# The second expert's second product as seven products of halves, with a new instruction order

## Chip, core and metric

The kernel runs on one core of one Trainium2 chip. The metric is device time in microseconds (us), the median of several executions. TensorE (PE in the rows) multiplies, with its weight loads shown apart as PEld; VectorE (DVE), ScalarE (ACT) and GpSimd (POOL) do the elementwise work; SyncE's queue (SP) issues every DMA.

## The reference

A linear attention without softmax, a root mean square norm over heads, and two feed-forward experts, one behind the other, over 4608 tokens of width 512. The first expert has an inner width of 2048, the second of 1024.

```
kv  = einsum('bhsd,bhse->bhde', k, v)
out = einsum('bhsd,bhde->bhse', q, kv)
x   = out / sqrt(mean(out*out) + 1e-6) * g_norm        # then to (4608, 512)
h   = x @ w_in;   x = (h * cos(h)) @ w_out             # first expert, d_ff 2048
h   = x @ w_in2                                        # second expert, d_ff 1024
e   = exp(h - max(h));  solu = h * e / (sum(e) + 1e-9)
ln  = (solu - mean) / sqrt(var + 1e-6) * g_ln
out = ln @ w_out2
```

All of it is fp32. The kernel splits each operand of a large product into a high part, rounded to the matmul's format, and a low part, the rest; `mm3` (lines 170 to 173) makes a product of three matmuls: high by high, high by low, low by high. Each matmul comes with a weight load of 128x128.

## The kernel before

**Products of halves.** Several products are made by seven products of halves in place of eight (Winograd's form): the left operand is cut into A11, A12, A22 and the sums S1 to S4, the right one into B11, B21, B22 and the sums T1 to T4, and the results are added from PSUM. Before the change this holds for the first expert's first product and for the second expert's first product (`second`), not for the second expert's second product (`second_out`).

**Stages.** Attention and a first quarter of the first expert run interleaved in blocks of 512 tokens (36 steps, `step_h` and `step_out`). Then the other three quarters of the first expert run in blocks of 3 or 4 tiles of 128 tokens per half (`first_h`, `first_out`), so that their moving operand has 384 or 512 columns. Meanwhile jobs (`job_in`, `job_out`, `job_b`, `job_lw`) decode the weights, which arrive as 64-bit words, split them and spill the parts to DRAM. Then comes the second expert, 18 pairs of tiles of 128 tokens:

- `prep_second` loads the pair and forms the sums of halves on POOL (`prep`), the high parts on ACT and the low parts on DVE.
- `second`: 42 matmuls of 512 columns, copied and added into `h2` by ACT and DVE.
- `soft`, for each of the two rows: maximum (DVE), exponential (ACT), product (DVE), square (ACT), a power on POOL, scaling (DVE).
- `second_out`, for each row: 8 transposes of 128 columns by TensorE, high parts on ACT (line 1017), low parts on DVE (line 1020), then 24 matmuls of 512 columns against `rg` 0 to 7, which hold the weights from `lwd`; one copy (ACT, line 1034) and one DMA out.

**What sets the order.** All work is given to a planner (`Flow`) as tasks with an engine, a duration, what they read and write, and a due time `at`. `Flow.run` lays them out in time by those numbers and emits each engine's instructions in that order. On the chip every engine runs its own list in order and waits on semaphores, so a duration in the table moves instructions, and a wait at the head of an engine's list holds all behind it.

```
s, eng = min((min(start(t) for t in q), e) for e, q in ready.items() if q)
t = min((t for t in q if start(t) <= s), key=lambda t: (t.at, t.seq))
t.end = self.free[eng] = s + t.dur
```

The code of the parts that the change touches:

Of the kernel before, what the change touches and what calls it, by code (L numbers as in the profile page):

```python
# [8 lines left out]
F32 = mybir.dt.float32  # L9
# [8 lines left out]
P = 128  # L18
# [27 lines left out]
POW = 2.0  # L46

BLOCKS = (0, 3), (6, 3), (12, 4), (20, 4), (28, 4)
E2_JOBS = (0, 0, 0, 0, 0, 0, 2, 3, 0, 2, 3, 0, 1, 1, 0)
PREP_LEAD, PREP_D, H_LATE, H_EARLY, JOB_AT = 12, 3, 0.3, 0.6, 10  # L50
T0, STEP_A, ITEM = 25.0, 8.0, 42.0
SLOTS0, SLOT_T, SLOT_D, SLOT_LATE, SLOT_RATE, JOB0, JOB1 = 8, -12, 1, -16, 2.0, 5, 32
CV_AHEAD, W_LOAD = 15, (-18.5, -12.5, -9, 6, 10, 14, 18, 22)
MM4, MM2 = 0.68, 0.36
GAP, PE_LAT = 0.04, 0.26
XPRI = 10
ATT_LEAD, CV_LEAD, Q_LEAD, PRI = 8, 14, 16, 20
KV_T = 0.62
PAIR_C, TR_LAG, OUT_LAG = 22.3, 20.0, 31.0
# [7 lines left out]
class Flow:  # L67
# [53 lines left out]
    def run(self):  # L121
        ready = {}
        port = 0.0

        def release(t):
            t.ready = 0.0
            for d in t.deps:
                gap = d.lat + (GAP if d.eng != t.eng or t.eng not in ("PE", "SP") else 0.0)
                if d.eng == "PE" and t.eng != "PE":
                    gap += PE_LAT  # L130
                t.ready = max(t.ready, d.end + gap)
            ready.setdefault(t.eng, []).append(t)

        def start(t):
            return max(self.free.get(t.eng, 0.0), t.ready, port if t.port else 0.0)
# [8 lines left out]
        for _ in self.tasks:  # L144
# [4 lines left out]
            t.end = self.free[eng] = s + t.dur  # L149
            if t.port:  # L150
                port = t.end
# [8 lines left out]
def tile_kernel(ctx, tc, qkv, tail, g2, w1, w2, gl, out):  # L160
# [26 lines left out]
    lwd = dram.tile([NC, P, 2, 512], F32, name="lwd")  # L187


    for key in ("g2", "halfpi"):  # L190
        declare("const", key, 0, [P, 1])
# [5 lines left out]
    declare("edge", "edge", 0, [P, 40])  # L197
    for s in range(2):
# [29 lines left out]
    declare("e2a", "xb", 2, [P, KC, TB])  # L228
# [9 lines left out]
    declare("e2t", "su", 6, [P, 512])  # L238
# [79 lines left out]
    def lhl(s):  # L318
        return buf["rwo", s].rearrange("p (l c n) -> p l c n", l=2, c=NC)
# [14 lines left out]
    hvs = Ring(("hv", i) for i in range(4))  # L334
    tts = Ring(("tt", i) for i in range(3))
# [16 lines left out]
    def convert(src, sk, yk, wk, at, load_at, on_dve, wide=1.3):  # L352
# [27 lines left out]
    def either(on_dve, n, fn, r, w, at):  # L380
        eng = DVE if on_dve else POOL
        dur = e_(0.82, 0.5, n) if on_dve else e_(1.38, 0.8, n)
        add("DVE" if on_dve else "POOL", dur, lambda: fn(eng), r=r, w=w, at=at)

    def split(src, keys, n, hi, lo, hk, lk, at, on_dve, scale=None):
# [8 lines left out]
        add("ACT", 0.64 if n == 512 else 0.42, lambda: ACT.copy(out=hi(), in_=src()), r=keys, w=hk, at=at)  # L394
# [91 lines left out]
    def kv_pair(b, bk, p, w, at):  # L486
# [12 lines left out]
        if b == 0:  # L499
            q_load(j, at + 3, Q_CUTS)  # L500
        add("PE", KV_T, mm, r=[kv, tl] + ([bk] if p % 2 else []), w=w + ([] if p % 2 else [bk]), at=at)

    def kv_slots(b):
        n, bks = ("kvf", b % 2), [att_bank() for _ in range(2)]

        def slot(half):
            def run(at):
# [4 lines left out]
                for e in range(2):  # L512
# [6 lines left out]
                    add("ACT", 0.35, copy, r=[bk, *done] + ([n] if half or e else []),  # L519
# [24 lines left out]
    def first_block(at, step):  # L544
# [4 lines left out]
        for p in range(NPAIR):  # L549
# [4 lines left out]
            for e in range(2):  # L554
                r, col = slice(e * D, (e + 1) * D), slice(p * P + e * D, p * P + (e + 1) * D)
                add("ACT", 0.26, lambda r=r, col=col, p=p: ACT.copy(
# [9 lines left out]
            add("PE", 0.45, mm, r=[kvf, ("kvfp", p, 0), ("kvfp", p, 1), q, ("qp", q, 0)], w=[bk], at=t)  # L566
            add("ACT", 0.61, lambda sq=sq, bk=bk: ACT.activation(out=buf[sq], in_=buf[bk], func=AF.Square, scale=D ** -0.5),
# [727 lines left out]
```

## Time and profile before

| | |
|---|---|
| median of 3 runs | 1279.22 us (1276.19 to 1279.84) |
| profiled execution, whole time | 1274.1 us |
| profiled execution, span of the core | 1272.3 us |
| mean granted TensorE clock | 0.999 |
| busy: PE, PEld, DVE, ACT, POOL | 98%, 83%, 72%, 53%, 40% |

The rows further down come from that one execution, whose whole time is 1.8 us above its span. A matmul's row shows its start and a modelled duration, which overlaps the next one; the distance from start to start says how fast they follow one another. A row's bracket names idle time before it and what ended it.

### The profile page before, as it was taken

Reading aid. Unit: us, or ns where it says so; the run is one execution under the profiler, and the core shown is the slowest. Engines: PE = TensorE matmul, PEld = TensorE weight load, DVE = VectorE, ACT = ScalarE, POOL = GpSimd, SP = SyncE. Lnnn points to the kernel's source line nnn. Section 1 sums busy time; section 2 is a strip of 40 time slices with the busy share of each in tenths; the row PEclk is TensorE's granted clock in tenths of the full one; section 3 lists DMA queues with packets and bytes.
Section 4 is the critical chain, followed back from the end, with each engine's and each line's share of the span. In section 5 each row is a group of like instructions: output and inputs, shape, how many; then the busy total and the mean of one; then the engine's idle time right before and its main releaser. Section 6 shows DMA issues by size and latency. Waiting matters only on the chain.

```text
span 1272.3 us, 18770 instructions
## 1 busy us (share of the span) xinstructions
PE 1241.3 (98%) x6576; PEld 1058.1 (83%) x6576; DVE 914.8 (72%) x1544; ACT 680.0 (53%) x1233; POOL 510.2 (40%) x510
## 2 busy tenths in 40 slices
PE   6799999999999999999999999999999999999998
PEld 4578888878999999888888888887888888888887
DVE  5777676787877777877788866656867776777753
ACT  4666766765564563555455534523655455455543
POOL 3237556665654764763463443322321212121000
PEclk9999999999999999999999999999999999999999
DMA  8779899577957857674865474396211111111000
GB/s 288 242 271 305 285 320 324 184 252 235 308 205 217 270 200 235 228 257 125 251 219 180 129 239 133 114 307 197 67 50 58 42 50 50 42 50 42 26 25 34
DMA packets 177407, 224.60 MB, mean 177 GB/s; under 512 B 11424, under 2 KB 114848, under 8 KB 177312
## 3 DMA queue, kind: packets, MB, share of 16 engines
q1 hardware_dynamic: 177312, 223.39, 54.0%
q8 instruction: 52, 0.85, 0.3%
q14 instruction: 43, 0.35, 0.1%
HBM read 156.77 MB, written 66.58 MB: 176 GB/s over the span
## 4 chain that ended last, share of the span: by engine, by line
PE 88%; DVE 3%; POOL 3%; DMA 2%; ACT 2%; issue 1%; SPq 0%; ACTq 0%; POOLq 0%; DVEq 0%
PE ps L171 27%; PE ps L173 27%; PE ps L172 27%; PE ps L1014 2%; PE ps L613 2%; POOL att L540 1%; PE ps L495 1%; DMA wid<-ws 1%; DMA px<-fh 1%; PE ps L645 1%; DMA att<-qkv 1%; POOL att L539 0%; POOL fconv L377 0%; POOL ws L395 0%; ACT xf L651 0%
## 5 line engine op out<-in xcount | busy, mean ns | idle before, releaser
L171 PE MATMUL ps<-rg,rwo 128*128 128x512 f32 (+1 forms) x912 | 347.2, 381 | 2.5 <-ACT fh L790 1.3
L173 PE MATMUL ps<-rg,rwo 128*128 128x512 f32 (+1 forms) x912 | 344.8, 378 | 1.2 <-DVE rwo L395 1.2
L172 PE MATMUL ps<-rg,rwo 128*128 128x512 f32 (+1 forms) x912 | 344.6, 378 | 1.0 <-DVE rg L755 1.0
L758 POOL TENSOR_TENSOR rg<-fh,rg 128x512 fp32r<-128x512 f32 (+1 forms) x120 | 146.0, 1230 | 141.9 <-ACT rg L753 124.7
L171 PEld LDWEIGHTS ps<-rg,rwo 128*128 128x128 f32 x912 | 171.2, 188 | 30.5 <-ACT fh L790 1.7
L173 PEld LDWEIGHTS ps<-rg,rwo 128*128 128x128 f32 x912 | 171.2, 188 | 30.0 <-DVE rwo L395 1.6
L172 PEld LDWEIGHTS ps<-rg,rwo 128*128 128x128 f32 x912 | 171.3, 188 | 28.9 <-DVE rg L755 1.3
L996 POOL TENSOR_TENSOR const<-const,const 128x1 f32<-128x1 f32 x36 | 21.1, 587 | 329.8 <-DVE const L993 244.9
L171 PE MATMUL ps<-rxa,rwi 128*128 128x512 f32 (+1 forms) x384 | 146.2, 381 | 1.4 <-DVE fh L944 0.9
L173 PE MATMUL ps<-rxa,rwi 128*128 128x512 f32 (+1 forms) x384 | 144.3, 376 | 0.0
L172 PE MATMUL ps<-rxa,rwi 128*128 128x512 f32 (+1 forms) x384 | 144.2, 376 | 0.0
L747 ACT ACTIVATE fh<-fh,const 128x512 f32<-128x512 f32 (+1 forms) x156 | 106.3, 691 | 40.0 <-DVE fh L744 39.3
L742 ACT ACTIVATE fh<-ps 128x512 int32<-128x512 f32 (+1 forms) x126 | 71.4, 568 | 104.6 <-PE ps L173 79.1
L171 PE MATMUL ps<-rxb,rwi 128*128 128x512 f32 (+1 forms) x288 | 110.8, 385 | 0.4 <-DVE fh L751 0.4
L172 PE MATMUL ps<-rxb,rwi 128*128 128x512 f32 (+1 forms) x288 | 108.4, 376 | 0.0
L173 PE MATMUL ps<-rxb,rwi 128*128 128x512 f32 (+1 forms) x288 | 108.3, 376 | 0.0
L744 DVE SCALAR_TENSOR_TENSOR fh<-ps,fh 128x512 f32<-128x512 f32 (+1 forms) x126 | 81.5, 648 | 29.6 <-ACT fh L742 27.8
L683 POOL TENSOR_TENSOR sf<-xf 128x256 f32<-128x256 f32 x72 | 63.8, 893 | 64.9 <-DMA xf<-xd 34.0
L890 DVE TENSOR_TENSOR mid<-ps,mid 128x512 f32<-128x512 f32 (+1 forms) x90 | 56.9, 635 | 43.7 <-PE ps L173 42.2
L395 POOL TENSOR_TENSOR ws<-fconv,ws 128x512 fp32r<-128x512 f32 (+1 forms) x52 | 65.9, 1271 | 44.8 <-ACT ws L394 40.2
L171 PEld LDWEIGHTS ps<-rxa,rwi 128*128 128x128 f32 x384 | 72.1, 188 | 13.2 <-DVE fh L944 1.4
L377 POOL TENSOR_TENSOR fconv<-fconv 128x512 f32<-128x512 f32 x40 | 53.3, 1333 | 73.8 <-DVE fconv L375 68.4
(134 smaller groups left out, 2377.1 us busy)
## 6 DMA issues: line engine op xcount, KB each, us to landing
rwi<-wid SPq DMA_DIRECT2D x66, 512.0 KB, 5.2
rwo<-wod SPq DMA_DIRECT2D x88, 256.0 KB, 3.5
fconv<-w SPq DMA_DIRECT2D x36, 512.0 KB, 5.4
att<-qkv SPq DMA_DIRECT2D x32, 512.0 KB, 6.7
px<-fh SPq DMA_DIRECT2D x42, 256.0 KB, 3.9
xd<-xf SPq DMA_DIRECT2D x18, 512.0 KB, 3.9
wid<-ws SPq DMA_DIRECT2D x18, 512.0 KB, 4.6
xf<-xd SPq DMA_DIRECT2D x18, 512.0 KB, 5.3
```

The costliest lines, as they stand in the source:

```text
L171: PE.matmul(ps, lhsT=lh, rhs=rh, start=start, stop=False, skip_group_check=more)
L172: PE.matmul(ps, lhsT=lh, rhs=rl, start=False, stop=False, skip_group_check=more)
L173: PE.matmul(ps, lhsT=ll, rhs=rh, start=False, stop=stop, skip_group_check=more)
L377: either(on_dve, 512, lambda eng: eng.tensor_tensor(out=buf[wk], in0=buf[yk], in1=buf[wk], op=ALU.add), r=[yk, wk], w=[wk], at=at)
L395: either(on_dve, n, lambda eng: eng.tensor_tensor(out=lo(), in0=src(), in1=f(hi()), op=ALU.subtract), [*keys, *hk], lk, at)
L613: PE.matmul(buf[bk][row:row + n, c], lhsT=buf[qs[p]][:, a:a + n], rhs=buf[kvf][:, c], start=True, stop=True)
L683: add("POOL", 0.9, lambda: POOL.tensor_tensor(out=out_(), in0=in0(), in1=in1(), op=fn), r=[*keys, *r], w=w, at=at)
L742: add("ACT", e_(0.61, 0.42, n), lambda: ACT.activation(out=tt().bitcast(I32), in_=h(), func=AF.Copy, scale=INV_2PI, bias=0.25), r=r, w=[tk ...
L744: add("DVE", e_(0.71, 0.44, n), lambda: DVE.scalar_tensor_tensor(out=tt(), in0=h(), scalar=INV_2PI, in1=tt().bitcast(I32), op0=ALU.mult, o ...
L747: add("ACT", e_(0.74, 0.5, n), lambda: ACT.activation(out=tt(), in_=tt(), func=AF.Sin, bias=buf["halfpi"][:, 0:1], scale=TWO_PI), r=[tk, " ...
L758: either(on_dve, n, lambda eng: eng.tensor_tensor(out=lo(), in0=g(), in1=f(hi()), op=ALU.subtract), [*gk, *hk], lk, t + 2)
L890: add("DVE", e_(0.71, 0.44, n), lambda ak=ak, bk=bk: DVE.tensor_tensor(out=buf[ak][:, 0:n], in0=buf[bk][:, 0:n], in1=buf[ak][:, 0:n], op=A ...
```

## The change

**The second product.** `second_out` now takes a pair of rows at once. The eight blocks of 128 of the inner dimension are cut into two halves of four, the columns into two halves of 256, and the two tiles of tokens are the halves of the rows. After the 16 transposes (as many as before) ACT copies one block of four from PSUM and DVE forms four sums S1 to S4 into buffers `e`; then seven operands get high parts (ACT) and low parts (DVE for A11, A12 and A22, POOL for the four sums). Seven products of 4 x 3 matmuls of 256 columns follow, 84 in all for 48 of 512 columns, and five adds (DVE) and two copies (ACT) of 256 columns put the result together.

**What feeds it.** `job_lw` makes the seven right-hand parts: 4 jobs for 8, each with two decodings, four scalings on ACT, the differences on POOL and four spills in place of two. The weights take 14 loads of 512 KB in place of 8, into `rg`, the new pool `e2r` and `ws`.

**Elsewhere.** The low parts in `prep_second` move from DVE to POOL; two small DVE operations of `soft` become one on ACT; one small ACT operation with a sine is put at the program's start and one with an exponential ahead of the second expert, each of which loads its table there.

**The order.** The planner's durations are set anew, most of them lower; `SLACK` multiplies them by 1.1 (DVE 1.11), `OVER` lets an operation start a little before the end of the one ahead, and POOL and DVE no longer exclude each other on the port but lengthen each other. Due times move too. All engines' lists change in all stages.

```diff
-PREP_LEAD, PREP_D, H_LATE, H_EARLY, JOB_AT = 12, 3, 0.3, 0.6, 10
+PREP_LEAD, PREP_D, H_LATE, H_EARLY, JOB_AT = 4.22, 3, 0.24, 0.31, 8.01
-MM4, MM2 = 0.68, 0.36
-GAP, PE_LAT = 0.04, 0.26
+MM4, MM2 = 0.68, 0.355
+GAP, PE_LAT, PORT = 0.04, 0.16, 0.58
+SLACK = {"DVE": 1.11, "ACT": 1.1, "POOL": 1.1}
+OVER = {"DVE": 0.084, "ACT": 0.104, "POOL": 0.042}
...
-            t.end = self.free[eng] = s + t.dur
+            t.end = s + t.dur * SLACK.get(eng, 1.0)
...
-             lambda part, lo, hi: e2xs(i)[:, part, 2 * lo:2 * hi, :], ("xsh", i), ("xsl", i), at, lambda n: True)
+             lambda part, lo, hi: e2xs(i)[:, part, 2 * lo:2 * hi, :], ("xsh", i), ("xsl", i), at, lambda n: False)
...
-        for c in range(NC):
-            add("PE", 0.7, lambda c=c: mm(c), r=[("lhq", n, c // 4), ("llq", n, c // 4), ("lw", c)] + ([bk] if c else []),
-                w=[bk], at=at)
...
+        add("ACT", 0.59, lambda: ACT.copy(out=total(S3), in_=a(1, 0)), r=[bks[1, 0]], w=[("sum", S3)], at=at)
+        op(S1, ALU.add, lambda: a(1, 1), lambda: total(S3), [("sum", S3), bks[1, 1]])
+        op(S3, ALU.subtract, lambda: a(0, 0), lambda: total(S3), [("sum", S3), bks[0, 0]])
+        op(S2, ALU.subtract, lambda: total(S1), lambda: a(0, 0), [("sum", S1), bks[0, 0]])
+        op(S4, ALU.subtract, lambda: a(0, 1), lambda: total(S2), [("sum", S2), bks[0, 1]])
+        for o in (A11, S2, S1, A12, S3, S4, A22):
+            if o in (A11, A12, A22):
+                nq = {A11: (0, 0), A12: (0, 1), A22: (1, 1)}[o]
+                src, keys, eng, dur = (lambda nq=nq: a(*nq)), [bks[nq]], "DVE", 0.69
+            else:
+                src, keys, eng, dur = (lambda o=o: total(o)), [("sum", o)], "POOL", 1.294
...
+                def mm(c=c):
+                    mm3(half(bk), xt(o, 0)[:, c, :], xt(o, 1)[:, c, :], lw(b, 0)[:, c, :], lw(b, 1)[:, c, :],
+                        c == 0 and not more, c == 3, more)
...
+    table(AF.Sin, -40)
...
+    table(AF.Exp, T_E2)
```

In the pieces of the order below, `ps_0_167` to `ps_0_195` are the eight PSUM banks, `rg`, `ws` and `e2r` hold weights of the second product, `rwo` and `e2r_7460` to `e2r_7462` its left operand, `rwi` the left and `rxa`, `rxb` the right operand of `second`, and `att` the attention's buffers. Lines 1014 and 1037 are the transposes of `second_out`, lines 171 to 173 and 179 to 181 the three matmuls of `mm3`.

TensorE's list in the steady part of the second expert, before, where the second product of a pair begins:

```order
L171 MATMUL ps_0_175<-rg_85,rwo_75 128x512 [waits Activation_49]
L172 MATMUL ps_0_175<-rg_85,rwo_75 128x512
L173 MATMUL ps_0_175<-rg_85,rwo_75 128x512
L171 MATMUL ps_0_175<-rg_86,rwo_75 128x512
L172 MATMUL ps_0_175<-rg_86,rwo_75 128x512
```

The same place after the change, where the product A11 by B11 begins and, further on, one whose low part comes from POOL:

```order
L179 MATMUL ps_0_187<-rg_85,rwo_75 128x256 [waits Activation_49]
L180 MATMUL ps_0_187<-rg_86,rwo_75 128x256
L181 MATMUL ps_0_187<-rg_85,rwo_75 128x256 [waits DVE_49]
...
L179 MATMUL ps_0_179<-rg_89,rwo_76 128x256 [waits DVE_49]
L180 MATMUL ps_0_179<-rg_90,rwo_76 128x256
L181 MATMUL ps_0_179<-rg_89,rwo_76 128x256 [waits Pool_49]
```

The matmuls have half the columns, and a third matmul of a group waits for POOL where no matmul of this product did before.

TensorE's list near the start, before, at the first use of the first expert's result (`rg_85`):

```order
L613 MATMUL ps_0_191<-att_152,att_146 64x128
L495 MATMUL ps_0_195<-att_138 64x64 [waits DMAHW0_49]
...
L171 MATMUL ps_0_175<-rg_85,rwo_75 128x512 [waits Activation_49]
L172 MATMUL ps_0_175<-rg_85,rwo_75 128x512 [waits DVE_49]
...
L613 MATMUL ps_0_191<-att_153,att_147 64x128
...
L613 MATMUL ps_0_195<-att_153,att_150 128x128
L171 MATMUL ps_0_167<-rxa_81,rg_91 128x512 [waits Activation_49]
```

The same place after the change:

```order
L640 MATMUL ps_0_191<-att_152,att_146 64x128
L522 MATMUL ps_0_195<-att_138 64x64 [waits DMAHW0_49]
...
L640 MATMUL ps_0_191<-att_153,att_147 64x128
...
L640 MATMUL ps_0_195<-att_153,att_150 128x128
L179 MATMUL ps_0_167<-rxa_81,rg_91 128x512 [waits DVE_49]
...
L179 MATMUL ps_0_175<-rg_85,rwo_75 128x512
```

The eight attention matmuls and twelve matmuls of `step_h` (`rxa_81`, `rg_91`) moved ahead of the first use of `rg_85`.

TensorE's list at the program's end after the change, from the last of `second` (`rxb_2481`) to the last pair's transposes and the first products behind them:

```order
L181 MATMUL ps_0_191<-rxb_2481,rwi_734 128x512
L179 MATMUL ps_0_179<-rg_91,rwo_76 128x256 [waits Activation_49]
...
L181 MATMUL ps_0_179<-ws_96,e2r_7462 128x256
L1037 MATMUL ps_0_183<-const_70,fconv_101 128x128 [waits DVE_49]
...
L1037 MATMUL ps_0_175<-const_70,fconv_101 128x128 [waits Activation_49]
...
L179 MATMUL ps_0_187<-rg_85,rwo_75 128x256 [waits Activation_49]
...
L179 MATMUL ps_0_187<-rg_87,rwo_75 128x256 [waits Activation_49]
...
L179 MATMUL ps_0_179<-rg_89,rwo_76 128x256 [waits DVE_49]
...
L181 MATMUL ps_0_179<-rg_89,rwo_76 128x256 [waits Pool_49]
```

Between the last matmul of `second` and the last transposes stand 72 matmuls of 256 columns, where before there were 48 of 512; between the transposes and the first product on a sum stand 18 of 256 columns.

## Rows read from the trace of the kernel before

**Rows 1.** The page: busy us, share of the span and instructions of each engine.

```profile
PE 1241.3 (98%) x6576; PEld 1058.1 (83%) x6576; DVE 914.8 (72%) x1544; ACT 680.0 (53%) x1233; POOL 510.2 (40%) x510
```

**Rows 2.** Six stretches: length, busy us of PE, PEld, DVE, ACT, POOL, granted clock, DMA, GB/s.

```profile
0.00:82.00 82.00, 61.14 (x496) 48.06 (x496) 58.29 (x103) 45.75 (x88) 26.75 (x30) 0.98 0.81 273
82.00:360.00 278.00, 273.06 (x1751) 234.06 (x1752) 205.60 (x333) 181.92 (x342) 169.14 (x163) 1.00 0.84 278
360.00:866.50 506.50, 506.50 (x2423) 442.84 (x2422) 370.70 (x595) 250.40 (x452) 241.20 (x218) 1.00 0.65 206
866.50:890.00 23.50, 22.55 (x104) 18.40 (x103) 16.85 (x31) 11.79 (x20) 7.35 (x10) 1.00 0.51 155
890.00:1244.00 354.00, 354.00 (x1695) 295.10 (x1694) 253.15 (x465) 180.90 (x317) 64.62 (x89) 1.00 0.14 45
1244.00:1272.30 28.30, 24.07 (x114) 19.59 (x112) 10.16 (x21) 9.28 (x16) 1.10 (x2) 1.00 0.10 38
```

**Rows 3.** TensorE's waits, whole span: us in total, times, longest.

```profile
PE ps L171 <- ACT rg L753: 1.1, 1, 1.1
PE ps L172 <- DVE rg L755: 1.0, 1, 1.0
PE ps L1014 <- DVE rwo L1020: 0.6, 1, 0.6
```

**Rows 4.** TensorE in the second expert, in order of time: start us, us.

```profile
1050.04 0.39 PE L173 MATMUL ps<-rg,rwo 128*128 128x512 f32 x1
...
1054.80 0.39 PE L173 MATMUL ps<-rg,rwo 128*128 128x512 f32 x1
1055.03 1.03 PE L1014 MATMUL ps<-const,fconv 128*128 128x128 f32 x8
1055.82 0.48 PE L171 MATMUL ps<-rxb,rwi 128*128 128x512 f32 x1
1056.13 0.40 PE L172 MATMUL ps<-rxb,rwi 128*128 128x512 f32 x1
```

**Rows 5.** TensorE in the first expert's blocks of three tiles, same columns.

```profile
329.82 0.33 PE L171 MATMUL ps<-rg,rwo 128*128 128x384 f32 x1
...
331.38 0.33 PE L171 MATMUL ps<-rxb,rwi 128*128 128x384 f32 x1
```

**Rows 6.** Weight loads in the second expert, same columns.

```profile
1053.21 0.19 PEld L173 LDWEIGHTS ps<-rg,rwo 128*128 128x128 f32 x1
...
1055.79 0.19 PEld L171 LDWEIGHTS ps<-rxb,rwi 128*128 128x128 f32 x1
1055.90 0.19 PEld L172 LDWEIGHTS ps<-rxb,rwi 128*128 128x128 f32 x1
```

**Rows 7.** TensorE, attention's matmuls of 64 columns, same columns.

```profile
88.86 2.55 PE L495 MATMUL ps<-att 128*64 128x64 f32 x80
```

**Rows 8.** Groups from 866.5 us on, shapes apart: busy us, mean ns, idle before.

```profile
L1020 DVE TENSOR_TENSOR rwo<-ps,rwo 128x512 fp32r<-128x512 f32 x72 | 47.7, 688 | 32.6 <-ACT rwo L1017 32.6
L1017 ACT CAST rwo<-ps 128x512 fp32r<-128x512 f32 x72 | 40.3, 594 | 14.2 <-PE ps L1014 14.2
L395 DVE TENSOR_TENSOR rwi<-sf,rwi 128x512 fp32r<-128x512 f32 x32 | 21.9, 690 | 0.0
L395 DVE TENSOR_TENSOR rwi<-xf,rwi 128x256 fp32r<-128x256 f32 x16 | 7.2, 450 | 0.0
```

**Rows 9.** A group of POOL, whole span, shapes apart.

```profile
L395 POOL TENSOR_TENSOR ws<-fconv,ws 128x512 fp32r<-128x512 f32 x42 | 58.0, 1385 | 23.3 <-ACT ws L394 18.7 <-issue 3.1 <-PE ps L173 1.3
```

**Rows 10.** ACT near the start: in the chain that ended last, and by time.

```profile
35.19 1.28 ACT L747
...
35.19 1.28 ACT L747 ACT_TABLE_LOAD   x1
```

**Rows 11.** The end of the program on DVE: start us, us.

```profile
1244.89 0.68 DVE L944 TENSOR_TENSOR fconv<-ps,fh 128x512 f32<-128x512 f32 x1
1252.41 0.81 DVE L998 TENSOR_SCALAR fconv<-fconv,const 128x1024 f32<-128x1024 f32 x1 [0.73 <-POOL const L996]
```

More of the change, by code (lines that the diff above doesn't have):

```diff
@@ L148, in run @@
             q.remove(t)
[L149 removed]
+            t.end = s + t.dur * SLACK.get(eng, 1.0)
             if t.port:
[L151 removed]
+                a, b = port.get("DVE" if eng == "POOL" else "POOL", (0.0, 0.0))
+                t.end += PORT * max(0.0, min(b, t.end) - max(a, s))
+                port[eng] = s, t.end
+            self.free[eng] = t.end - OVER.get(eng, 0.0)
             t.fn()
@@ L334, in tile_kernel @@
     hvs = Ring(("hv", i) for i in range(4))
+    ovs = Ring(("ov", i) for i in range(4))
     tts = Ring(("tt", i) for i in range(3))
@@ L393, in split @@
             return
-        add("ACT", 0.64 if n == 512 else 0.42, lambda: ACT.copy(out=hi(), in_=src()), r=keys, w=hk, at=at)
+        add("ACT", 0.62 if n == 512 else 0.405, lambda: ACT.copy(out=hi(), in_=src()), r=keys, w=hk, at=at)
         either(on_dve, n, lambda eng: eng.tensor_tensor(out=lo(), in0=src(), in1=f(hi()), op=ALU.subtract),
@@ L517, in copy @@
                                  in_=buf[bk][r, 0:P].rearrange("p (n w) -> p n w", w=D))
-                    add("ACT", 0.35, copy, r=[bk, *done] + ([n] if half or e else []),
+                    add("ACT", 0.26, copy, r=[bk, *done] + ([n] if half or e else []),
                         w=[("kvfh", n, half, e)] + ([] if half or e else [n]), at=at)
@@ L789, in block_out @@
             place, pk = px_place(4 * m, 1, 4, d)
-            add("ACT", 0.6, lambda sk=sk, bk=bk: ACT.copy(out=buf[sk], in_=buf[bk]), r=[bk], w=[sk], at=at)
+            add("ACT", 0.59, lambda sk=sk, bk=bk: ACT.copy(out=buf[sk], in_=buf[bk]), r=[bk], w=[sk], at=at)
             add("SP", 0.8, lambda sk=sk, place=place: SP.dma_start(
@@ L850, in first_h @@
         prod(bA, A11, B11, at)
-        add("ACT", e_(0.6, 0.39, n), lambda: ACT.copy(out=buf[v0][:, 0:n], in_=buf[bA][:, 0:n]), r=[bA], w=[v0],
+        add("ACT", e_(0.59, 0.366, n), lambda: ACT.copy(out=buf[v0][:, 0:n], in_=buf[bA][:, 0:n]), r=[bA], w=[v0],
             at=at + d + E_)
@@ L950, in second @@
         prod(bA, A11, B11)
-        add("ACT", 0.6, lambda: ACT.copy(out=buf[v0], in_=buf[bA]), r=[bA], w=[v0], at=at)
+        add("ACT", 0.59, lambda: ACT.copy(out=buf[v0], in_=buf[bA]), r=[bA], w=[v0], at=at)
         prod(bB, S2, T2)
@@ L957, in second @@
         place, keys = to_h(0, 0)
-        add("ACT", 0.6, lambda: ACT.copy(out=place(), in_=buf[bA]), r=[bA], w=keys, at=at)
+        add("ACT", 0.59, lambda: ACT.copy(out=place(), in_=buf[bA]), r=[bA], w=keys, at=at)
         prod(bB, S3, T3)
```

280 lines of the change are left out of this document (168 added, 112 removed).

## The prediction

> **What bounds the kernel now.** I read the page first: TensorE is busy for 1241.3 us of a span of 1272.3 us, no other engine for more than 72% [rows 1]. The stretches then show where the missing 31 us lie: 20.9 in the first 82 us, 4.9 up to 360 us, none up to 866.5, 1.0 and 0.0 in the second expert up to 1244, and 4.2 at the end [rows 2]. So from 360 us on only TensorE's own time counts, and at the start the chain of waits does. The clock is granted in full (1.00, which is 2.4 GHz) in all but the first stretch.
>
> A matmul's row overlaps the next, so I take its price from starts. In the second expert 21 steps of 512 columns take 1054.80 - 1050.04 = 4.76 us, or 0.2267 us each; eight transposes take 0.79 us, and the matmul behind them comes 0.31 after the first, 0.08 late, so a transpose costs 0.110 us [rows 4]. With 384 columns nine steps take 1.56 us, or 0.1733 [rows 5]. Check: a pair has 90 matmuls of 512 columns and 16 transposes, 20.40 + 1.76 = 22.16 us, 18 pairs 398.9 us; the second expert runs from 866.5 us to the end, and TensorE is busy there for 22.55 + 354.00 + 24.07 = 400.6 us [rows 2]. The sum holds to 1.7 us.
>
> **The second product's matmuls.** Removed: 48 x 0.2267 = 10.88 us a pair. Added: 84 matmuls of 256 columns, a width that the trace does not show. The two widths shown differ by 0.0533 us for 128 columns; by the same step 256 columns take 0.120 us, 10.08 a pair. That saves 0.80 us a pair and **14.4 us** over 18. What could break the line is the weight load, one for each matmul: two loads pressed together start 0.11 us apart [rows 6], so 0.110 is the floor (84 x 0.110 = 9.24, 29.5 us saved in all), and 0.120 leaves only 0.010 us of cover. Issue is no limit: 80 small matmuls with their loads take 2.55 us, 0.032 each [rows 7]. The upper end is the nearest row, 0.1733 [rows 5], by which a pair would lose 3.68 us, 66 in all. I take 0.120, since above the floor the step per column is straight between 384 and 512 and nothing else in the rows grows.
>
> A load's row lasts 0.19 us, but one starts at 1053.21 and the next matmuls still follow at 0.2267 us, which is 512 columns at 2.4 GHz (0.2133) and 0.0133 more: the load lies beside the matmul ahead of it [rows 4, 6]. The Trainium skill, "TensorE: Matmul & The Clock Gate", section "The mechanism" in Part 3, says that a load overlaps matmuls in flight only when it targets another row group; every load here covers all rows, so by that rule load and matmul would add up. The trace disagrees: at 512 columns the two would make 0.2133 + 0.110 = 0.323, not 0.2267. By the rule the 84 matmuls would take 0.107 (256 columns at 2.4 GHz) + 0.110 each, 18.2 us a pair against 10.08 by the rows; it is the last of the rivals below.
>
> **The helpers in the second expert.** Per pair of 22.16 us the steady stretch gives DVE 253.15/354 x 22.16 = 15.8 us, ACT 11.3, POOL 4.0 [rows 2]. DVE loses the low parts of the preparation (3 x 0.69 + 0.45), four of the second product (4 x 0.688) and some 0.6 of small operations, 5.9 in all, and gains seven operations of 0.688 and five of about 0.45, 7.1: 17.0 of the new 21.36 us. ACT loses six of 0.594 and gains eight of that, two of half width at about 0.4 and two small ones, so 13.7 at most. POOL gains 3 + 4 low parts of 1.385 and one of half width, about 0.7: 14.4 us [rows 8, 9]. All stay below 81% of a pair, so TensorE hides them: nothing. If that cover goes, each us by which a helper is late in every pair costs 18 us. As these lists are fixed, and TensorE's third matmul of a group now waits for POOL with all later matmuls behind it, I put down **+1 us** of waits (from 0 to 5).
>
> **Weights.** Six more loads of 512 KB are 3.1 MB at the second expert's start, where 155 GB/s are moved now against 273 to 278 in the early stretches [rows 2]: 11 to 20 us. They are first used behind two `second` and 16 transposes, 84 x 0.2267 + 1.76 = 20.8 us in. Hidden, at 0 to 5 us if late; I take 0. The added decoding work falls between 360 and 866 us, where POOL is busy for 241 of 506 us and ACT for 250: about 20 low parts and differences more, hidden: 0.
>
> **The end.** Last sum of `second` to last scaling: 1244.89 to 1252.41 + 0.81, 8.3 us of `soft` [rows 11]. Before, 48 x 0.2267 = 10.9 us of matmuls cover it. After, 72 x 0.120 = 8.6 do, and the sum starts 0.3 to 0.8 behind the last matmul: a wait of about 0.4. Then S1 takes a copy, a sum, a high part and a low part, 0.59 + 0.69 + 0.59 + 1.39 = 3.3 us and the hops, begun 0.4 before the last transpose ends, against 18 x 0.120 = 2.2 us of matmuls: about 1.0. Before there is one wait of 0.6 [rows 3, 8, 9]. Net **+1.0 us** (0 to 3).
>
> **The order before the second expert.** This is the part that arithmetic reaches least. On the chain of waits at the start lies a table load of 1.28 us ahead of the first sine [rows 10]; it moves to where ACT has nothing: -1.3, with less if the next wait takes its place. TensorE now waits 1.1 and 1.0 us at the first use of `rg_85` with others behind it that could run [rows 3]; the new list has eight small ones and twelve of 0.2267 ahead of it, over 2.7 us of cover. So up to 3.4 us at one place. But DVE is busy for 58.3 of the first 82 us and feeds what TensorE waits for [rows 2], so part comes back as a later wait. The idle time up to 360 us is 25.8 us [rows 2], of which I take half as the most that lists alone can win; in the other direction, new waits of about 1 us, like those in the rows, at eight places would cost 8. I take **-3.5 us** (-12 to +8).
>
> **Sum.** -14.4 + 1.0 + 1.0 - 3.5 = -15.9 us: a span of 1256.4 and, with 1.8 us around it, 1258.2 for the profiled execution. That of before lay 5.1 us below the median of its runs (1274.1 against 1279.22), so I forecast 1279.2 - 15.9, rounded to **1263 us**.
>
> **Rivals.** *The new order gives more*: the idle time before 360 us falls by some 12 and the matmuls of 256 columns come nearer to the floor, at 0.118: 2.7 more. Then 1263 - 8.5 - 2.7 = 1252, down to 1248. For it speaks that the waits there are many and short; against it DVE's share.
>
> *A helper paces the second expert* (the other side). POOL goes from 4.0 to 14.4 us a pair, and its low parts hold the third matmul of `second` and of four products. The gain is gone when a pair takes 22.16 us again, so when TensorE waits 0.8 us more in each. At 1 us it costs 18: 1281; at 2 us 1299, slower. Against it: POOL's mean of 1.385 is from stretches in which DVE is as busy as here.
>
> *The new order loses before the second expert*, by 8 rather than gaining 3.5: 1274.5.
>
> *The change doesn't do what it says*: the load cannot be hidden behind 256 columns. From 0.1295 us a matmul on the product saves nothing; if it is not hidden at all, 0.107 + 0.110 = 0.217, a pair takes 84 x 0.217 - 10.88 = 7.3 us more, 132 in all: 1263 + 14.4 + 132 = 1409. Against it is the pace at 512 columns [rows 4].
>
> **Chances.** Forecast 0.62 (its own range 1256 to 1270); more from the order 0.15; a helper paces 0.13, of which 0.05 still faster, 0.03 the same, 0.05 slower; the order loses 0.08 (0.04, 0.03, 0.01); loads not hidden 0.02, slower. A difference of 0.3%, 3.8 us, is about what a measurement can tell, so faster means below 1275.4 and slower above 1283.1: 0.86, 0.06, 0.08. The range from 1248 to 1275 leaves out the far end of the second case and the slow ones, under 0.2.
>
> **What will show it.** Starts of the 256-column matmuls 0.118 to 0.122 us apart; pairs of about 21.4 us, so some 393 us from the first matmul of `second` to the end of the span, not 405.8; TensorE's waits on POOL lines below 2 us in all; no table load in the chain at the start; idle time in the first 82 us below 20.9; 1 to 2 us of waits between the last transposes and the last products. I am wrong if weight loads stand further apart than 0.120, if POOL or ACT heads the list of releasers within the second expert, or if idle time before 360 us grows.

## The result, and the profile after the change

The changed kernel took 1265.38 us, the median of four runs (1264.59 to 1268.83), against 1277.91 for four of the kernel before (1276.19 to 1279.84): a ratio of 0.9907, interval 0.9881 to 0.9932. A second set of the unaltered kernel (`e5` below) gave 1267.24 against 1274.97, 0.9934 (0.9914 to 0.9954). So it is faster by some 8 to 13 us (about 1%), half to four fifths of the forecast 15.9. The profiled execution is the slowest of the first four, 1268.83 with a span of 1267.0.

The page's busy times of the changed kernel, and under them the same stretches as [rows 2] (the last ends 5.3 us earlier):

```profile
PE 1231.0 (97%) x7224; PEld 1079.5 (85%) x7224; DVE 960.8 (76%) x1537; ACT 725.3 (57%) x1366; POOL 725.1 (57%) x686
```

```profile
0.00:82.00 82.00, 66.67 (x528) 54.64 (x529) 65.56 (x116) 50.40 (x98) 27.53 (x32) 1.00 0.86 287
82.00:360.00 278.00, 270.65 (x1751) 232.99 (x1750) 217.32 (x338) 183.33 (x344) 182.12 (x174) 1.00 0.87 289
360.00:866.50 506.50, 498.89 (x2365) 433.33 (x2364) 363.75 (x560) 255.41 (x464) 272.09 (x245) 1.00 0.64 204
866.50:890.00 23.50, 23.50 (x106) 19.45 (x105) 12.38 (x19) 9.38 (x18) 12.65 (x14) 1.00 0.88 267
890.00:1244.00 354.00, 353.75 (x2347) 322.81 (x2345) 290.49 (x484) 219.03 (x429) 224.52 (x217) 1.00 0.15 47
1244.00:1267.00 23.00, 17.58 (x137) 16.26 (x136) 11.29 (x23) 7.73 (x15) 6.15 (x6) 1.00 0.12 47
```

In the second expert POOL's added work costs nothing: from 890 to 1244 us it is busy for 224.5 of 354 us instead of 64.6, and TensorE for all but 0.25. The idle time of TensorE went from 20.9 to 15.3 us in the first stretch, but from 4.9 to 7.4 in the second, and from 0.0 to 7.6 between 360 and 866.5 us, where the kernel before had none [rows 2].

Two times split the result. The first matmul of the second expert starts at 866.52 us before and at 872.94 after, 6.4 us **later**; from there to the end of the span it is 405.8 us before and 394.1 after, 11.7 us **shorter**. What was forecast for the second part was 12.4 (14.4 less 2), and for the first part a gain of 3.5.

TensorE's timeline of the changed kernel, inside a run of the second product (start, duration):

```profile
1005.82 0.28 PE L179 MATMUL ps<-rg,rwo 128*128 128x256 f32 x1
1005.94 0.28 PE L180 MATMUL ps<-rg,rwo 128*128 128x256 f32 x1
...
1009.06 0.28 PE L179 MATMUL ps<-rg,rwo 128*128 128x256 f32 x1
```

27 steps take 3.24 us: 0.120 us for a matmul of 256 columns, as drawn from the widths of 384 and 512. And TensorE's waits from 872.9 us to the end, all of them (us in total, times, longest):

```profile
PE ps L179 <- ACT fh L1086: 1.2, 1, 1.2
PE ps L179 <- DVE fh L1082: 0.6, 1, 0.6
PE ps L179 <- ACT fconv L1049: 0.2, 1, 0.2
PE ps L1037 <- DVE fconv L1025: 0.2, 1, 0.2
```

No POOL line is among them. The last of the four is in the first pair, at 894.6 us; the other three, 2.0 us, are at the end, behind the last pair's transposes. What has to be explained is the stretch from 360 to 866.5 us. TensorE's timeline at its longest wait there:

```profile
630.04 0.39 PE L181 MATMUL ps<-rxa,rwi 128*128 128x512 f32 x1
634.57 0.50 PE L179 MATMUL ps<-rxb,rwi 128*128 128x512 f32 x1 [4.13 <-DVE fh L866]
...
635.37 0.43 PE L179 MATMUL ps<-rxb,rwi 128*128 128x512 f32 x1
635.60 0.62 PE L180 MATMUL ps<-rxb,rwi 128*128 128x512 f32 x1
636.02 0.63 PE L181 MATMUL ps<-rxb,rwi 128*128 128x512 f32 x1
...
639.01 0.40 PE L179 MATMUL ps<-rxa,rwi 128*128 128x512 f32 x1
```

The first four starts behind the wait still stand 0.33 to 0.23 apart; from 635.60 to 639.01 us eight steps take 3.41 us, 0.43 each instead of 0.2267: 512 columns at 1.2 GHz. The windows' row says the same of the clock (the column behind the engines is the granted clock):

```profile
634.50:639.00 4.50, 4.43 (x12) 3.50 (x13) 4.38 (x7) 2.46 (x4) 1.28 (x1) 0.62 0.93 298
```

Eight steps with 0.2 us too much each are 1.6 us, so the wait costs 5.7 us with what follows it. Who was late is read backwards, from DVE to POOL to ACT (timeline rows of these engines):

```profile
633.83 0.68 DVE L866 TENSOR_TENSOR fh<-ps,fh 128x512 f32<-128x512 f32 x1
```

```profile
632.44 1.47 DVE L400 TENSOR_SCALAR fconv<-fconv 128x512 uint32<-128x512 uint32 x1 [4.00 <-POOL ws L422]
```

```profile
631.69 0.72 POOL L422 TENSOR_TENSOR ws<-fconv,ws 128x256 fp32r<-128x256 f32 x1 [9.21 <-ACT ws L421]
```

```profile
631.20 0.40 ACT L421 CAST ws<-fconv 128x256 fp32r<-128x256 f32 x1 [4.09 <-DMA lwd<-ws]
```

The sum that TensorE waits for (L866) stands behind the next decoding's L400 in DVE's list; L400 overwrites a buffer that POOL still has to read for the last split of the job before (L422); that split has no room, since there are two `ws` rooms and the spill `lwd<-ws` of one is not down yet. The planner gives a spill 2.0 us to land; the three of this stretch took 3.7 to 4.9. The one waited for took 4.9, and left at 626.23 us, 3.7 after POOL had written its room.

### The profile page after: what moved, and what is told of

Its sections match the earlier page's. It is cut to its first block, busy times and chain, and to the rows that moved or that the text cites. A ratio compares the mean times of both kernels' runs of the same rounds, so it can differ in the third digit from the quotient of the medians.

```text
span 1267.0 us, 20461 instructions
## 1 busy us (share of the span) xinstructions
PE 1231.0 (97%) x7224; PEld 1079.5 (85%) x7224; DVE 960.8 (76%) x1537; ACT 725.3 (57%) x1366; POOL 725.1 (57%) x686
## 4 chain that ended last, share of the span: by engine, by line
PE 79%; DMA 6%; DVE 6%; POOL 4%; ACT 3%; issue 2%; SPq 0%; POOLq 0%; ACTq 0%; DVEq 0%
PE ps L180 24%; PE ps L179 24%; PE ps L181 24%; PE ps L1037 2%; PE ps L640 2%; DMA xf<-xd 2%; PE ps L522 1%; DMA px<-mid 1%; POOL rg L785 1%; DMA px<-fh 1%; PE ps L672 1%; POOL fconv L446 1%; DVE rxb L422 1%; PE ps L590 1%; DVE fconv L397 1%
## 5 line engine op out<-in xcount | busy, mean ns | idle before, releaser
L179 PE MATMUL ps<-rg,rwo 128*128 128x512 f32 (+2 forms) x912 | 315.9, 346 | 1.5 <-ACT fh L1086 1.2
L180 PE MATMUL ps<-rg,rwo 128*128 128x512 f32 (+2 forms) x912 | 314.1, 344 | 1.6 <-POOL rg L785 1.6
L181 PE MATMUL ps<-rg,rwo 128*128 128x512 f32 (+2 forms) x912 | 314.2, 344 | 0.1
L785 POOL TENSOR_TENSOR rg<-fh,rg 128x512 fp32r<-128x512 f32 (+1 forms) x120 | 150.2, 1261 | 173.2 <-ACT rg L780 169.2
L180 PEld LDWEIGHTS ps<-rg,rwo 128*128 128x128 f32 x912 | 172.2, 189 | 20.9 <-POOL rg L785 2.6
L422 POOL TENSOR_TENSOR ws<-fconv,ws 128x512 fp32r<-128x512 f32 x68 | 84.2, 1243 | 52.6 <-ACT ws L421 33.5
L422 POOL TENSOR_TENSOR rwi<-sf,rwi 128x512 fp32r<-128x512 f32 x36 | 52.3, 1453 | 57.0 <-ACT rwi L421 56.1
L780 ACT CAST rg<-fh 128x512 fp32r<-128x512 f32 (+1 forms) x120 | 68.5, 576 | 26.7 <-DVE fh L778 26.0
```

The costliest lines, as they stand in the source:

```text
L179: PE.matmul(ps, lhsT=lh, rhs=rh, start=start, stop=False, skip_group_check=more)
L180: PE.matmul(ps, lhsT=lh, rhs=rl, start=False, stop=False, skip_group_check=more)
L181: PE.matmul(ps, lhsT=ll, rhs=rh, start=False, stop=stop, skip_group_check=more)
L422: either(on_dve, n, lambda eng: eng.tensor_tensor(out=lo(), in0=src(), in1=f(hi()), op=ALU.subtract), [*keys, *hk], lk, at)
L780: add("ACT", e_(0.62, 0.405, n), lambda: ACT.copy(out=hi(), in_=g()), r=gk, w=hk, at=t + 2)
L785: either(on_dve, n, lambda eng: eng.tensor_tensor(out=lo(), in0=g(), in1=f(hi()), op=ALU.subtract), [*gk, *hk], lk, t + 2)
```

## The experiments

All are compared with the kernel before, run beside them. The last two columns are of each profiled execution: the first matmul of the second expert, and the time from it to the end of the span. A profiled execution is one of those behind the median: it lies 3.5 us above it for the changed kernel's first profile, and 0.4 to 4.7 us below it for `e2`, `e3`, `e5` and `e8`.

| run | median | before | ratio (interval) | second expert at | takes |
|---|---|---|---|---|---|
| before, first profile | | | | 866.5 | 405.8 |
| changed, first profile | 1265.38 | 1277.91 | 0.9907 (0.9881-0.9932) | 872.9 | 394.1 |
| `e5` changed, again | 1267.24 | 1274.97 | 0.9934 (0.9914-0.9954) | 867.3 | 394.2 |
| `e1` second expert alone | 1310.31 | 1274.99 | 1.0273 (1.0256-1.029) | 879.0 | 431.5 |
| `e2` order alone | 1270.08 | 1274.99 | 0.9966 (0.9953-0.9979) | 862.4 | 405.5 |
| `e3` low parts on DVE | 1269.88 | 1274.99 | 0.9954 (0.9936-0.9972) | 864.3 | 399.0 |
| `e4` no sine table | 1267.41 | 1274.99 | 0.9944 (0.9927-0.9961) | 871.0 | 393.5 |
| `e6` second expert, new port rule | 1286.14 | 1274.97 | 1.0078 (1.0048-1.0107) | 882.0 | 401.3 |
| `e7` spills in ACT's queue | 1267.29 | 1274.97 | 0.9938 (0.9918-0.9959) | 870.5 | 394.2 |
| `e8` 4.5 us for the sums to land | 1261.37 | 1274.97 | 0.9881 (0.9861-0.9901) | 862.0 | 395.2 |
| `e9` T4 second | 1269.6 | 1275.23 | 0.9955 (0.9941-0.997) | 876.6 | 393.5 |
| `e10` 4.5 us for sums and spills | 1268.56 | 1275.23 | 0.9946 (0.9928-0.9964) | 873.7 | 393.6 |
| `e11` products left out | 1195.64 | 1275.23 | one run | 869.8 | 323.7 |
| `e12` 128 columns | 1253.46 | 1274.3 | one run | 866.1 | 385.6 |

### The two halves of the change

**e2, the order alone.** The planner, its durations and due times and the sine table as changed; `second_out`, `job_lw` and what else belongs to the second expert as before.

> The new planner, durations, due times and the sine table at the start, with the second expert and its weights as before. Theory (the order gains about 5.6 us in the first 82 us and loses as much again between 82 and 866 us): 1274 to 1280 us, no difference that can be told from before; idle time of TensorE in the first 82 us near 15 us, and up to the first matmul of the second expert no gain. Rival (the order gives what was forecast, or more): 1270 to 1274 us, or below. Other rival (the order loses, as the profiled execution of the changed kernel shows with 6.4 us): 1281 to 1286 us.

4.9 us faster (2.7 to 6.0 by the interval), and the second expert begins 4.1 us earlier: the forecast was 3.5. The theory that the order gives back all it gains is wrong, and the rival holds. Its waits of TensorE from 400 us to the second expert are all of these:

```profile
PE ps L179 <- DVE fh L847: 0.5, 1, 0.5
PE ps L179 <- DVE fh L759: 0.3, 1, 0.3
PE ps L180 <- POOL rg L766: 0.2, 1, 0.2
```

So the 4 us wait of the changed kernel comes with the other half; the rows above lead to its new decoding jobs.

**e1, the second expert alone.** The seven products, what feeds them, the low parts on POOL, laid out by the old planner with its durations and due times, but for three due times of the second expert (`PAIR_C`, `TR_LAG`, `OUT_LAG`), which are those of the changed kernel.

> The second expert as changed (seven products of halves, what feeds them, the low parts on POOL, the exponential table ahead of it), laid out by the planner, durations and due times of before; no sine table at the start. Theory (the second product saves about 12 us, the new order next to nothing): the second expert takes 394 us from its first matmul to the end, as in the changed kernel, against 405.8 before, and the whole 1264 to 1268 us. Rival (the product needs the new order, or the new order gave a large part): 1272 us or more, with waits of TensorE within the second expert of over 4 us.

35 us **slower**. The miss is of my theory, and the rival holds: the product is not worth 12 us by itself. The second expert already begins 12.5 us late (879.0 against 866.5), and the rest is lost within it, where TensorE waits above all for the ends of `soft` and for copies:

```profile
PE ps L1029 <- DVE fconv L1017: 14.7, 9, 6.6
PE ps L171 <- ACT fconv L979: 9.4, 9, 1.8
```

**e6, the same with one rule of the planner.** POOL and DVE no longer exclude each other, but lengthen each other, as in the changed kernel:

```diff
-            return max(self.free.get(t.eng, 0.0), t.ready, port if t.port else 0.0)
+            return max(self.free.get(t.eng, 0.0), t.ready)
...
-                port = t.end
+                a, b = port.get("DVE" if eng == "POOL" else "POOL", (0.0, 0.0))
+                t.end += PORT * max(0.0, min(b, t.end) - max(a, s))
+                port[eng] = s, t.end
```

> The second expert as changed, laid out by the durations and due times of before, but with the new rule of the planner by which POOL and DVE may lie side by side and lengthen each other. With the old rule it took 431.5 us instead of 394. Theory (the old rule counts POOL's 14.4 and DVE's 7.2 us a pair in SBUF one after the other, more than a pair has, so that its lists run out of step with the chip): the second expert comes back to 394 to 400 us and the whole to 1268 to 1278 us. Rival (durations or due times did it): it stays above 415 us and the whole above 1290 us.

Of the 37.4 us that `e1` loses in the second expert against the changed kernel, this rule gives back 30.2: 401.3 us. Before that stretch it gains nothing (882.0), so the whole stays slower than before; both times lie past the ends of the ranges that I gave. In the second expert TensorE's longest waits shrink to:

```profile
PE ps L1032 <- DVE fconv L1020: 3.0, 1, 3.0
PE ps L176 <- DVE rwo L1056: 2.1, 1, 2.1
PE ps L174 <- ACT rwo L1055: 0.8, 1, 0.8
```

That the rule decides it, with the old durations, is shown. The reason that I expected, that 14.4 us on POOL and 7.2 on DVE one behind the other are more than a pair has, fits, but is argued from the counts.

### What holds TensorE near 630 us

**e5, the changed kernel again.**

> The changed kernel once more, unaltered, so that the next three have it beside them. The profiled execution of the first run reached the second expert 6.4 us later than before, though its median fell by 12.5. Theory (the four added decoding jobs hold DVE behind the spills in SP's queue, every time): a wait of 3 to 4 us near 625 to 630 us with TensorE at half its clock behind it, the first matmul of the second expert at 868 to 873 us. Rival (a chance of that one execution): no wait of more than 1.5 us between 570 and 700 us, and the second expert begins by 864.

The wait is there each time, behind 624 us here, with the clock at 0.60 behind it:

```profile
628.86 0.50 PE L179 MATMUL ps<-rxb,rwi 128*128 128x512 f32 x1 [4.14 <-DVE fh L866]
```

```profile
628.70:633.00 4.30, 4.14 (x11) 3.27 (x12) 4.30 (x7) 2.46 (x4) 1.28 (x1) 0.60 1.01 318
```

The profiles of `e3`, `e4`, `e11` and `e12`, which do not touch this place, show it too, with 3.3 to 3.7 us. But the second expert begins at 867.3 here instead of 872.9. Of these 5.7 us, 2.4 are there already at the first matmul of 512 columns (18.51 against 20.95 us), while the first loads arrive; the rest gathers in short waits up to 516 us, the longest of 1.3 us. So runs of one list differ by that much, and the theory's 868 was missed by a little. A difference of less than 6 us in the column "second expert at", which is from one execution each, thus counts only where something else shows it too.

**e7, the spills in ACT's queue.**

```diff
+        queue, eng, cost = ("ACT", ACT, 0.1) if done[0][0] == "lwd" else ("SP", SP, 0.8 * n / 512 + 0.1)
...
-        add("SP", 0.8 * n / 512 + 0.1, lambda: SP.dma_start(out=to(), in_=f(ws(i)[:, :, 0:n])),
+        add(queue, cost, lambda: eng.dma_start(out=to(), in_=f(ws(i)[:, :, 0:n])),
```

> The changed kernel, with the spills of the second product's weights issued from ACT's queue instead of SP's. Theory (these spills stand in SP's queue behind loads that wait for writes to land, which holds `ws`, then POOL, then DVE, then TensorE): the wait near 625 to 630 us and the half clock behind it go, 3.5 to 6 us; the second expert begins 4 to 6 us earlier than in the unaltered kernel, 1260 to 1262 us. Rival (it is the amount of decoding work on DVE and POOL that is late): the wait stays, and the time is that of the changed kernel to 2 us.

A miss: taking the spills out of SP's queue does not end the wait. Counted back from TensorE's wait, the spill now leaves some 4 us earlier (7.5 us ahead of it instead of 3.8), and TensorE still waits 4.6 us for the same sum; ACT's waits from 400 to 866 us for these landings rise from 4.1 and 4.6 us in the changed kernel's two profiles to 14.9:

```profile
ACT ws L421 <- DMA lwd<-ws: 14.9, 4, 7.4
```

**e9, T4 second.** The split that holds DVE's buffer is moved ahead of two others:

```diff
+        if done[0] == "lwd":
+            put(lambda: t(ka, 1), [ka], T4, 256)
         put(lambda: buf[kz], [kz], T1, 512)
         put(lambda: buf[kb], [kb], T3, 512)
-        put(lambda: t(ka, 1), [ka], T4, 256)
+        if done[0] != "lwd":
+            put(lambda: t(ka, 1), [ka], T4, 256)
```

> The changed kernel, in which the four decoding jobs of the second product's weights split and spill T4 second instead of last. T4 is the last reader of the buffer that the next decoding overwrites (line 400), and its split waited near 630 us for a `ws` room of a spill that took 3.6 to 6 us to land. Theory (DVE stands still at line 400 because the last split waits for a room): the wait of about 4 us with the half clock behind it goes or falls below 1.5 us, and the time is 3 to 5 us less than in the changed kernel, 1262 to 1264 us. Rival (any of the four would stand there, since the two rooms are too few): the wait stays within 1 us of 4 us, perhaps at another place, and 1266 to 1268 us.

The rival in kind, though its figures were low (the wait 3 to 5 us, the time to 1268): L400 is free, but TensorE waits 5.3 us behind 636.6 us for ACT instead, in whose list the next splits stand, waiting for the same rooms:

```profile
634.64 0.62 ACT L421 CAST ws<-fconv 128x512 fp32r<-128x512 f32 x1 [3.35 <-DMA lwd<-ws]
...
639.49 0.62 ACT L421 CAST ws<-fconv 128x512 fp32r<-128x512 f32 x1 [3.18 <-DMA lwd<-ws]
```

**e8, a longer time for the sums to land.** One number of the planner (line 921):

```diff
-                    r=[ak], w=pk, at=t - 2, lat=1.6)
+                    r=[ak], w=pk, at=t - 2, lat=4.5)
```

> The changed kernel, with the planner's time for the writes of partial sums to land (line 921) at 4.5 us instead of 1.6; the rows show 3.3 to 5.4. The loads that wait for them then stand behind the spills in SP's list. Theory: as with the spills in another queue, the wait near 630 us goes and the time falls to 1260 to 1263 us. Rival (a later load is late itself, since the sums wait for it): a wait on the sums (line 917) of the same size takes its place, 1265 us or more.

The time is the theory's: 1261.37 us, 5.9 below `e5` beside it, and the second expert begins at 862.0, where that of `e2` (862.4) begins without any of the new jobs. All of TensorE's waits from 400 us to there:

```profile
PE ps L179 <- ACT fh L878: 1.0, 2, 0.5
PE ps L179 <- DVE fh L866: 0.6, 2, 0.4
PE ps L179 <- DVE fh L778: 0.6, 2, 0.4
```

ACT waits longer for the rooms than in the changed kernel, 9.5 us in five waits against 4.1 and 4.6, but at places where DVE, at L400, waits at most 0.9 us behind it instead of 4.0, and TensorE at most 0.4:

```profile
ACT ws L421 <- DMA lwd<-ws: 9.5, 5, 3.6
```

So the decoding work was not too much; it stood at a bad place. The theory's reason is not shown, though. The one number moved the jobs as a whole: their 16 spills leave from 492.9 to 624.3 us instead of 529.5 to 672.9 (count, least, median and longest ns of the issue, first and last start in us; the changed kernel, then `e8`):

```profile
L429 SPq DMA_DIRECT2D lwd<-ws x16: 512/558/611, 529.5 to 672.9; - x16
L429 SPq DMA_DIRECT2D lwd<-ws x16: 513/554/1136, 492.9 to 624.3; - x16
```

Which of these moves ends the wait stays open. This version beats both kernels.

**e10, the same for spills and the first quarter's sums too.** Beside the edit of `e8`:

```diff
-            r=[("ws", i), ("wsl", i)], w=done, at=at, lat=2.0)
+            r=[("ws", i), ("wsl", i)], w=done, at=at, lat=4.5)
...
-                out=place(), in_=parted(buf[sk], 4)), r=[sk], w=pk, at=at, lat=1.6)
+                out=place(), in_=parted(buf[sk], 4)), r=[sk], w=pk, at=at, lat=4.5)
```

> The changed kernel with 4.5 us as the planner's time for three kinds of writes to land: the sums (lines 921 and 819, 1.6 before) and the weights' spills (line 430, 2.0 before). With the sums of line 921 alone it took 1261.4 us. Theory (the planner's lists fit the chip the better, the nearer its landing times are to those in the rows): the wait near 630 us stays away, the waits for DVE between 200 and 310 us fall from 6.3 to 7.4 to 3 to 5, and 1257 to 1261 us. Rival (the order between 82 and 310 us is bound by DVE, not by landing times): 1260 to 1263 us, no less than with line 921 alone.

A miss: some 7 us worse than `e8`. The wait near 630 us stays away, but at 328 us a new one of 6.4 appears. ACT waits for a weight's load that leaves at 325.4 us (at 323.6 in `e8`), and DVE and TensorE behind it; another, of 3.9, stands at 290 us:

```profile
331.62 0.66 ACT L393 ACTIVATE fconv<-fconv 128x512 f32<-128x512 f32 x1 [6.30 <-DMA fconv<-w]
```

```profile
PE ps L179 <- DVE fh L866: 6.4, 1, 6.4
PE ps L180 <- DVE rxb L422: 3.9, 1, 3.9
```

So numbers nearer to the rows do not make a better list as such: here two new waits took back what `e8` had gained.

### The helpers and the weight load

**e3, the low parts of the preparation back on DVE.**

```diff
-             lambda part, lo, hi: e2xs(i)[:, part, 2 * lo:2 * hi, :], ("xsh", i), ("xsl", i), at, lambda n: False)
+             lambda part, lo, hi: e2xs(i)[:, part, 2 * lo:2 * hi, :], ("xsh", i), ("xsl", i), at, lambda n: True)
```

> The changed kernel with the low parts of the preparation of the second expert back on DVE. Theory (the helpers have room to spare, and the move to POOL neither was needed nor costs anything): DVE goes from some 17.4 to 20 of the 21.4 us of a pair, the second expert stays at 394 to 396 us and the whole at 1264 to 1268 us. Rival (DVE is then the bound): TensorE waits for DVE in every pair; at 0.5 us each 1274 us, at 1 us 1283 us.

The second expert takes 399.0 us, 4.9 more than in the changed kernel; DVE is busy for 310.8 of 340 us from 900 to 1240 us (278.1 in `e5`), and TensorE waits for it and for ACT:

```profile
PE ps L1037 <- DVE fconv L1025: 2.3, 2, 1.8
PE ps L179 <- ACT fh L1086: 1.6, 5, 0.5
```

At 91% DVE begins to show, neither hidden in full nor the bound of every pair: both expectations were off. The medians, 1269.88 and 1267.24 in different runs, do not tell the two kernels apart by their intervals; the place does.

**e11, meant for 128 of the 256 columns.**

> The changed kernel, with only the first 128 of the 256 columns in every matmul of the second product; the other half of its columns is left out. It shows how near the weight load is to being the bound. Theory (the load of 0.110 us lies beside the matmul and is the floor): these matmuls start 0.110 to 0.115 us apart, 84 x 0.007 = 0.6 us a pair less, the second expert 380 to 392 us. Rival (no such floor; the step of 0.0533 us for 128 columns goes on): 0.067 us apart, 4.4 us a pair less, with TensorE waiting for DVE, which has 17 us of work a pair. Other rival (load and matmul add up, and 0.1196 was 0.107 and a small load): 0.066 or below.

The edit cut more than that: the seven products fell out entirely, with their additions, copies and the writing of the output; transposes, sums and splits stayed. So it tells nothing of the load. It does tell what the rest needs: 323.7 us, 18.0 a pair, with TensorE waiting for DVE's sums of `second` in every pair:

```profile
PE ps L179 <- DVE fconv L973: 32.5, 18, 2.4
PE ps L179 <- DVE fh L973: 26.4, 22, 2.6
```

By an estimate from these two numbers, of the changed kernel's 394.1/18 = 21.9 us a pair the helpers have less than 4 to spare, since their part of the products is missing here.

**e12, 128 of the 256 columns.**

```diff
-                    mm3(half(bk), xt(o, 0)[:, c, :], xt(o, 1)[:, c, :], lw(b, 0)[:, c, :], lw(b, 1)[:, c, :],
+                    mm3(half(bk)[:, 0:128], xt(o, 0)[:, c, :], xt(o, 1)[:, c, :], lw(b, 0)[:, c, 0:128], lw(b, 1)[:, c, 0:128],
```

> The changed kernel, with only the first 128 of the 256 columns in every matmul of the second product (the other 128 are left out); the run before it that was meant to do this left out the seven products with their additions, and took 323.7 us for the second expert. Theory (the weight load lies beside the matmul ahead of it, and 0.110 us is the floor): these matmuls start 0.110 to 0.115 us apart, 0.4 to 0.8 us a pair less, the second expert 380 to 390 us. Rival (no such floor; the step of 0.0533 us for 128 columns goes on): 0.067 us apart, where the seven products end by 5.6 us of TensorE's 10.9, and the helpers, which need about 18 us a pair without the products, set the pace: 325 to 345 us for the second expert.

TensorE's timeline within a second product:

```profile
1003.55 0.27 PE L181 MATMUL ps<-e2r,e2r 128*128 128x128 f32 x1
1003.66 0.27 PE L179 MATMUL ps<-e2r,e2r 128*128 128x128 f32 x1
...
1007.24 0.28 PE L181 MATMUL ps<-ws,e2r 128*128 128x128 f32 x1
```

33 steps in 3.69 us, 0.112 each: half the columns save 7% of the time. That is close to the 0.110 at which two loads pressed together start [rows 6], and the second expert takes 385.6 us, within the theory's 380 to 390. The rule of the Trainium skill that the prediction weighed ("TensorE: Matmul & The Clock Gate", section "The mechanism" in Part 3) would add load and matmul here too, 0.053 + 0.110 = 0.163; the trace disagrees again. Another place of the same page ("Step-by-step: what each phase is for" in Part 2) says that loads are also pulled ahead of matmuls in flight when they go to a background weight buffer; that agrees with the pace here.

### The table at the start

**e4, no sine at the program's start.**

```diff
-    table(AF.Sin, -40)
```

> The changed kernel without the small sine at the program's start, so that the first real sine loads its table again. Theory (the load lies on the path at the start and costs its 1.3 us): the first 82 us get 1 to 1.3 us more idle time of TensorE, the whole 1266 to 1267 us. Rival (the wait that stood behind the load takes its place, and the gain of 5.6 us in the first 82 us is the order's alone): idle time of 15 to 15.5 us as in the changed kernel, and 1265 us.

The median, 1267.41 us, is not to be told from that of `e5` (1267.24). The place shows it nevertheless. ACT's and TensorE's timelines without the small sine:

```profile
33.28 1.28 ACT L774 ACT_TABLE_LOAD   x1
```

```profile
34.39 0.49 PE L640 MATMUL ps<-att,att 128*64 128x128 f32 x3
37.13 1.74 PE L640 MATMUL ps<-att,att 128*64 128x128 f32 x12 [2.25 <-ACT att L543]
```

and TensorE's with it, in `e5`:

```profile
34.56 0.49 PE L640 MATMUL ps<-att,att 128*64 128x128 f32 x3
35.88 1.74 PE L640 MATMUL ps<-att,att 128*64 128x128 f32 x12 [0.83 <-ACT att L543]
```

The load stands ahead of the copies that TensorE waits for, and costs 1.4 us there (2.25 against 0.83), as the theory says. At the first matmul of 384 columns 0.5 us of it is left (291.3 against 290.8 us), less than two executions of one list differ by, so how much of it stays is not shown.

## Why the prediction was right, and where not

The time (1263, range 1248 to 1275) and the sign held, but the gain was 8 to 13 us of the forecast 15.9. The two large terms came out near their sizes; what is missing is in the main one term that was set to nothing, and without it `e8` gains 13.6. Luck has a part in the number: the forecast starts from 1279.2 us, the median of three runs, and the later sets of the kernel before gave 1274.3 to 1275.2. From 1275 the same sum ends at 1259, so beside `e5`'s 1267.24 a base too high by 4 hid half of the 8 us by which the gain fell short.

- **Matmuls of 256 columns: right.** 0.120 us, and the second expert 11.7 us shorter against 12.4. The weight loads stay hidden, with 0.008 to 0.010 us to spare (`e12`); the rival of 1409 us is out. (At 0.118 us a pair would have saved 84 x 0.002 us more, 3.0 over 18 pairs; the first rival's 2.7 is a slip.)
- **Helpers: right.** One wait of 0.2 us between 872.9 us and the last pair, against +1. POOL paces nothing, and neither does DVE, with 290.5/354 x 21.4 = 17.6 us a pair against 17.0 forecast; `e3` and `e11` show that the room was small.
- **The weights' loads: right.** TensorE waits for none of them; all but four leave by 874.1 us, the first into `rg` at 852.3, 20 us ahead of the second expert. The estimate itself was too low: with 155 of 278 GB/s in use, 3.1 MB in what is left take 25 us, not 11 to 20.
- **The end: right in size, wrong in place.** 2.0 us of waits against 0.6 before [rows 3], so +1.4 (forecast +1.0, 0 to 3). But the wait on S1's parts is 0.2 instead of 1.0; 1.8 come between the last seven products, which wait for the copy and the sum that read their bank (L1086, L1082).
- **The order: right when alone.** 3.5 forecast, 4.1 in the profile and 4.9 by median in `e2`; the table load in it, 1.3 forecast, is 1.4 at its place (`e4`). But the prediction gave the order no part in the second expert, and it has one: with the old durations, the new second expert loses 30 us without the new port rule (`e1`, `e6`), so the gain of the product belongs to both. No rival had that.
- **"The added decoding work ..., hidden: 0": the step that failed.** It went by busy shares of POOL and ACT. Rooms and landings are not in those: with two `ws` rooms and spills of 3.7 to 4.9 us, the jobs stop DVE or ACT, and the sum behind. It costs 5.7 us at one place, in both profiles; the second expert begins at 867.3 and 872.9 us instead of 862.4 in `e2`. `e8` undoes it with the same work, 5.9 us by median. With the old order it seems to cost more: in `e1` the second expert begins 12.5 us later than before the change, and what differs ahead of it is in the main the decoding. So the whole change gains 7.7 us in `e5`, where the order alone gains 4.9 in `e2`.
- **What would show it wrong.** Idle time before 360 us did not grow (25.8 to 22.7); it grew behind 360 us, where I had not looked.

What stays open: what makes two executions of one list differ by 5.7 us up to the second expert (`e5`), beyond the 2.4 in which the first loads arrive; which of the moves in `e8` ends the wait; and whether a third `ws` room would end it, which was not tried.

## What to carry to other kernels

Work that a busy share shows as hidden can still stop the chain, if it stands in an in-order list and waits for a room: ask for each added job which rooms it needs, how long its transfers take to land by the rows, and what stands behind it. Two parts of a change, each timed alone, can miss by far what they do together: here one was 35 us slower and the other 5 faster alone, and both together 8 to 13 faster. Narrower matmuls pay only down to the width at which the load still hides: here 256 columns just, 128 not.

## What the hardware showed

- A matmul of 128 columns with its load follows at 0.112 us (`e12`), one of 256 at 0.120. From 512 to 256 the step is 0.0533 us for 128 columns; below that it is 0.008, with the start of a load every 0.11 us.
- After a wait of 4.1 us TensorE went on at 2.4 GHz for 1 us, then stood at 0.43 us per 512 columns (1.2 GHz) for 3.4 us, then at 0.2267 again: this wait cost 1.6 us beyond its length.
- Beside POOL's operation of 632.37 to 633.63 us, DVE's at L400 took 1.47 us (in the rows of the wait near 630 us), against 0.43 in `e7`, at 626.56 us, with POOL idle.
